# Splitting every second unit's probabilities in filled steps, with ScalarE and GpSimd sharing the work

## The chip, the cores and the metric

The kernel runs on one core of a Trainium2 chip. The metric is the device time of one execution in microseconds (us); the median of three runs is given, lowest and highest beside it. Engines go by the names of the profile: PE is TensorE with its matmuls, PEld its weight loads, DVE is VectorE, ACT is ScalarE, POOL is GpSimd, SP is SyncE, which issues most of the DMAs.

## What is computed

Two layers, each an attention block and a gated feed-forward block with a residual, over 2048 tokens of 448 features. The attention has 16 query heads of 28 features and one head of keys and values that they share. Inputs and output are f32.

```python
def _A_ref(x, wq, wk, wv, wo):
    B, S, D = x.shape
    H = 16
    Dh = D // H
    q = (x @ wq).reshape(B, S, H, Dh).transpose(0, 2, 1, 3)
    k = x @ wk
    v = x @ wv
    scores = jnp.einsum("bhqd,bkd->bhqk", q, k) * (Dh ** -0.5)
    p = _softmax(scores, axis=-1)
    o = jnp.einsum("bhqk,bkd->bhqd", p, v)
    return o.transpose(0, 2, 1, 3).reshape(B, S, H * Dh) @ wo

def _B_ref(x, w_gate, w_up, w_down):
    g = jnp.einsum("bsd,df->bsf", x, w_gate)
    u = jnp.einsum("bsd,df->bsf", x, w_up)
    return jnp.einsum("bsf,fd->bsd", _sigmoid(g) * u, w_down)

x = A_x
for _ in range(2):
    x = x + _A_ref(_layernorm(x, axis=-1), A_wq, A_wk, A_wv, A_wo)
    x = x + _B_ref(_layernorm(x, axis=-1), B_w_gate, B_w_up, B_w_down)
```

## The kernel before

**Tiles and steps.** The queries are cut into 16 tiles `u` of 128 rows, the keys into 16 tiles `kt` of 128 rows. A step, or unit, is one pair (u, kt) with all 16 heads: a layer has 256 of them. The heads go in four groups `g` of four. For a unit, four times (once for each group): a score matmul on PE (line 565) into a PSUM tile `s`, and an exponential on ACT (line 569) into an SBUF tile `P` of 128 keys by 512 (four heads of 128 queries), in f32. Then the PV matmuls of the unit (function `pv`) add the values, weighted by `P`, to one PSUM tile `pv`, whose four quarters of 32 rows belong to the four groups; the four groups' matmuls stand at different column positions of the array. Row 28 of a quarter gets the sum of the probabilities, since a column of the values is one.

**Two forms of PV.** Most units go through the f32 form: one f32 matmul for each group (line 583; the chip's records have two for each). Some units are split: each `P` is written as a sum of two f16 parts, high and low, made by `convert`. GpSimd makes the high part by a copy to f16 (line 602) and the low part by subtracting it from `P` (line 603); both go into a tile `PH`. PV is then three f16 matmuls for each group (line 579): high by high, high by low and low by high of probabilities and values; the values are split once for each layer (`VH`). Splitting is marked by the lists `KS` and the number `FROM`: a unit is split if its kt is 0, 4, 8 or 12, if 80 steps are past, and if the current order is FULL.

**Orders.** The engines get their instructions in an order that is written out by hand. A string of letters makes two steps:

```python
FULL = "FSFSFSFSTPPXMFSFSFSFSFXM"
LEAN = "FSFSmFSFSPTXmFSFSmFSFSPTXm"
```

S is a score and its exponential, followed by a call of `convert` for the tile marked before; P is the PV of the oldest waiting unit, if more than one waits; M is a group of mx work, which finds the maxima for a tile of queries ahead (four matmuls of line 508 and four reductions on DVE, line 511); F is a slice of filler work: the feed-forward block of earlier tiles (lines 369 and 787, with a tanh on ACT, line 750, a copy on ACT, line 761, and two operations on DVE, lines 758 and 762), projections for the next layer, the output projection (line 696). X moves the step on and runs short side chains, such as the normalisation of a finished tile of queries (GpSimd's multiplication of line 674 by `lb`, which comes back by DMA). FULL is used while enough filler work is left (more than 600 units of cost a step), LEAN else. In FULL the first half (up to PP) has an even kt, the second half an odd one, and both PV of the string stand together in the middle, so a unit is used up one string after its scores. What follows calls one FULL string a filled order.

**Buffers.** `P` tiles of kt divisible by four come from a pool of four (tag PX), the others from a pool of eight (tag P). Scores, mx and all filler accumulators share seven PSUM banks. The pool `big` has five SBUF tiles of 128 by 7 by 512 in f16, which hold the inputs of the projections and, early on, weights in preparation.

Behind each layer's last step comes a tail with the feed-forward block of the last tiles.

Of the kernel before, what the change touches and what calls it, by code (L numbers as in the profile page):

```python
# [8 lines left out]
F32 = mybir.dt.float32  # L9
F16 = mybir.dt.float16  # L10
I32 = mybir.dt.int32
AF = mybir.ActivationFunctionType
OP = mybir.AluOpType
# [6 lines left out]
def interleaved_layers_kernel(ctx: ExitStack, tc: tile.TileContext, x, wq, wk, wv, wo, wg, wu, wd, out, layers=2):  # L20
# [6 lines left out]
    nc = tc.nc  # L27
# [3 lines left out]
    NT, NB, G, KT, FC = S // 128, S // 512, H // 4, S // 128, F // 128  # L31
    U = NT
    TB, WB, HB = 2, 4, 8
    PB, PX = 8, 4
    HP = 2
    KS = (0, 4, 8, 12)
    FROM = 80
    CA = "PPPP"
    NBL = NT // TB
    EPS = 1e-5  # L40

# [3 lines left out]
    big = ctx.enter_context(tc.tile_pool(name="big", bufs=5))  # L45
    lay = ctx.enter_context(tc.tile_pool(name="lay", bufs=2))
    wk1 = ctx.enter_context(tc.tile_pool(name="wk1", bufs=2))
# [38 lines left out]
    def flush(every=False):  # L86
        todo, pend[:] = pend[:], []
        for i, (due, fn) in enumerate(todo):
            if due > now[0] and not every:
                pend.append((due, fn))  # L90
            else:
                fn()
        if every and pend:
            flush(True)
# [285 lines left out]
    KK, VV, VH, QH = {}, {}, {}, {}  # L380

    def layer_tiles(l):
        KK[l] = lay.tile([128, 2, S], F16, tag="KK", name="KK")
        VV[l] = lay.tile([128, KT, 32], F32, tag="VV", name="VV")
        nc.vector.memset(VV[l][:, :, 28:32], 0.0)
        nc.vector.memset(VV[l][:, :, 28:29], 1.0)
        VH[l] = lay.tile([128, 2, KT // HP, 32], F16, tag="VH", name="VH", bufs=1)
# [61 lines left out]
    def qgen(l, b):  # L449

        XT = XTQ.pop((l, b))
        for g in range(G):
            yield from qproj(l, XT, b, g)
        flush(True)
# [99 lines left out]
    def finish():  # L554
        while late:
            late.pop(0)()

    def group(m):
        next(m, None)
        next(m, None)  # L560

    def scores(l, u, kt, g, P):
        assert ("m", l, u) in stored, (l, u, kt)
        s = psf.tile([128, 512], F32, tag=BANKS["s"], name="s", bufs=NBK[BANKS["s"]])
        nc.tensor.matmul(s, KK[l][0:96, 0, kt * 128:(kt + 1) * 128], QS[l, u][:, g].rearrange("p h n -> p (h n)"),  # L565
                         start=True, stop=True)
        p = (wk1.tile([128, 512], F32, tag="P", name="P", bufs=PB) if kt % 4 else
             wk1.tile([128, 512], F32, tag="PX", name="P", bufs=PX))
        nc.scalar.activation(p, s, AF.Exp, scale=ESC)  # L569
        P.append(p)  # L570

    def pv(l, u, kt, P):
        if kt == 0:
            PVS[l, u] = psv.tile([128, 512], F32, tag="v", name="pv")
        v = PVS[l, u]
        if P[0].dtype == F16:
            for n, (a, c) in enumerate(((0, 0), (1, 0), (0, 1))):
                for g in range(4):
                    nc.tensor.matmul(v[32 * g:32 * g + 32], VH[l][:, a, kt // HP], P[g][:, c], start=kt + n == 0,
                                     stop=kt == KT - 1 and n == 2, tile_position=(0, 32 * g))  # L580
        else:
            for g in range(4):
                nc.tensor.matmul(v[32 * g:32 * g + 32], VV[l][:, kt], P[g], start=kt == 0, stop=kt == KT - 1,  # L583
                                 tile_position=(0, 32 * g))
        if kt == KT - 1:
            o = wk1.tile([128, 512], F32, name="pvs", bufs=1)
            nc.scalar.copy(o, v)
            PVS[l, u] = o


    def value_parts(l):
        nc.scalar.copy(VH[l][:, 0], VV[l][:, 0:KT:HP])
        nc.vector.tensor_tensor(VH[l][:, 1], VV[l][:, 0:KT:HP], VH[l][:, 0], op=OP.subtract)

    conv = []

    def convert():
        while conv:
            P, g = conv.pop(0)
            p, e = P[g], CA[g]  # L600
            h = wk1.tile([128, 2, 512], F16, name="PH", bufs=PX)
            {"A": nc.scalar.copy, "V": nc.vector.tensor_copy, "P": nc.gpsimd.tensor_copy}[e](h[:, 0], p)  # L602
            nc.gpsimd.tensor_tensor(h[:, 1], p, h[:, 0], op=OP.subtract)  # L603
            P[g] = h

    XTQ, BLK = {}, {}
    side = []
# [1 line left out]
    def later(*stages):  # L609

        side.append([stages[0][0], list(stages)])

    def tick():

        for s in list(side):
            s[0] -= 1
            if s[0] <= 0:
                flush()
                fill.run(s[1].pop(0)[1]())
                if s[1]:  # L620
                    s[0] = s[1][0][0]
                else:
                    side.remove(s)
# [287 lines left out]
    def warmth(n):  # L911
        p = psf.tile([128, 128], F32, tag="f", name="sca", bufs=NBK["f"])
        for _ in range(n):
            nc.tensor.matmul(p, one, one, start=True, stop=True)
# [209 lines left out]
    for n in range(4 * NB):  # L1124
        kb, g = divmod(n, G)
# [14 lines left out]
    FULL = "FSFSFSFSTPPXMFSFSFSFSFXM"  # L1140
    LEAN = "FSFSmFSFSPTXmFSFSmFSFSPTXm"
    PLAG = 1
# [8 lines left out]
    for l in range(layers):  # L1151
        mx = mxs[l]
        final = l + 1 == layers
        if not final:
            layer_tiles(l + 1)
        if l:
            for b in range(2, NB):
                fill.add(qgen(l, b), G * QCH)
        fill.slice(QCH)
        flush(True)  # L1160
        finish()
        group(mx)
        fill.slice(QCH)
        if l == 0:
            warmth(8)
        rate = 0.0
        PQ = []
        step = 0
        P = []
        sn = 0  # L1170
        while step < U * KT:
            order = FULL if rate > LEANR else LEAN
            for o in order:
                u, kt = divmod(step, KT)
                if o == "S":
                    su, skt = divmod(sn // 4, KT)
                    if sn < 4 * U * KT:
                        scores(l, su, skt, sn % 4, P)
                        convert()
                        if order is FULL and skt in KS and l * U * KT + step >= FROM and (sn % 4 == 0 or PARTS[0]):  # L1180
                            PARTS[0] = sn % 4 < 3
                            conv.append((P, sn % 4))
                        sn += 1
                        if sn % 4 == 0:
                            PQ.append((l, su, skt, P))
                            P = []
                elif o == "M":
                    group(mx)
                elif o == "m":
                    next(mx, None)  # L1190
                elif o == "T":
                    finish()
                elif o == "P":
                    convert()
                    if len(PQ) > (sn % 4 == 0) * PLAG:
                        pv(*PQ.pop(0))
                elif o == "X":
                    if u == 0 and kt in MORE:
                        group(mx)
                    if u and kt == 1:  # L1200
                        b = (u - 1) // TB
                        if (l, b) not in BLK:
                            BLK[l, b] = Block(l, b)
                        later(*BLK[l, b].tile(u - 1))
                    if step == 20:
                        value_parts(l)
                    if l == 0:
                        paced(step)
                    tick()
                    fed = sum(BLK[l, b].fed == TB for b in range(NBL) if (l, b) in BLK)  # L1210
                    if fed < NBL - 1:
                        rate = fill.left / max(FIRST + TB * KT * fed - step, 1)
                    else:
                        rate = max(fill.left - KEEP, 0) / (U * KT - step)
                    step += 1
                else:
                    fill.slice(rate * 2 / order.count("F"))
        convert()
        while PQ:
            pv(*PQ.pop(0))  # L1220
        flush(True)
        later(*BLK[l, NBL - 1].tile(U - 1))
        if not final:
            mxs[l + 1] = mx_gen(l + 1)
        n = done = 0
        many = 0 if final else 4 * NB + 1
        while side or pend or fill.first or done < many or final and fill.gens:
            tick()
            for _ in range(4):
                fill.slice(VS / 4)  # L1230
            n += 1
            if done < many and QDONE.get((l + 1, 0)) == G and mx_ready(l + 1, done) and (n >= EACH or done >= 4 * (NB - 1)):
                group(mxs[l + 1])
                done += 1
                n = 0
# [21 lines left out]
```

## Time and profile before

| | us |
|---|---|
| median of 3 runs (lowest, highest) | 2263.57 (2260.12, 2267.22) |
| the profiled execution's own time | 2260.52 |
| its span | 2258.7 |
| exponentials on ACT, line 569, 2048 of 599 ns | 1141.4 |
| mx reductions on DVE, line 511, 2048 of 680 ns | 1266.0 |
| score matmuls on PE, line 565, 2048 of 381 ns | 743.2 |

A row of the profile's groups names the line, the engine, the operation and the tile (out<-in), then the shapes, the count, the busy time in us, the mean of one in ns, and the idle time of the engine just before it with what ended it. A row of the waits names who waited for whom, the total in us, how many times, and the longest. A row of the timeline has the start, the length and the instruction; equal neighbours are merged and counted. Matmuls are pipelined and overlap in the records, so the time from one start to the next tells more of PE than the length of one.

### The profile page before, as it was taken

How to read it: one execution, taken by the hardware profiler on the slowest of the kernel's cores; microseconds unless marked ns; L12 is line 12 of the kernel's file. 1: busy time of each engine (PE TensorE's matmuls, PEld its weight loads, DVE VectorE, ACT ScalarE, POOL GpSimd, SP SyncE). 2: the span in 40 equal slices, each digit the busy share in tenths (PEclk: the TensorE clock that was granted, in tenths of full speed). 3: DMA queues.
4: the chain of work that ended last, by engine and by line, in shares of the span. 5: the costliest groups of instructions: out<-in, count | busy, mean ns of one | idle time of the engine just before them, and what ended most of it. 6: DMA issues, size and time to landing. Idle time of an engine off the chain costs nothing. (4 is left out here: it accounts for less than half of the span.)

```text
span 2258.7 us, 43078 instructions
## 1 busy us (share of the span) xinstructions
PE 2203.9 (98%) x16340; PEld 1048.8 (46%) x16340; DVE 1671.8 (74%) x2921; ACT 1397.9 (62%) x2568; POOL 1054.1 (47%) x1370
## 2 busy tenths in 40 slices
PE   8999999999999999999999999999999999999999
PEld 6312354444545454454573224445454544445457
DVE  7899887877778787774558887878787877878322
ACT  4677776666656666667325676666666666666631
POOL 5378452454454555556301015555545555555530
PEclk9999999999999999999999999999999999999999
DMA  6734642313323132323341113223222313232243
GB/s 160 214 98 132 203 141 62 107 62 99 112 64 99 61 98 72 99 95 89 101 137 53 29 51 108 79 85 101 65 91 67 103 57 99 78 95 89 78 108 113
DMA packets 224400, 217.53 MB, mean 96 GB/s; under 512 B 154048, under 2 KB 185536, under 8 KB 224192
## 3 DMA queue, kind: packets, MB, share of 16 engines
q1 hardware_dynamic: 217200, 198.89, 30.1%
q0 software_dynamic: 3680, 12.09, 1.4%
q10 hardware_dynamic: 3312, 3.79, 0.5%
q8 instruction: 128, 2.10, 0.4%
q14 instruction: 80, 0.66, 0.1%
HBM read 175.37 MB, written 23.59 MB: 88 GB/s over the span
## 5 line engine op out<-in xcount | busy, mean ns | idle before, releaser
L569 ACT ACTIVATE P<-s 128x512 f32<-128x512 f32 x2048 | 1141.4, 599 | 570.2 <-PE s L565 549.5
L511 DVE TENSOR_REDUCE mp<-mx 128x1 f32<-128x512 f32 x2048 | 1266.0, 680 | 308.3 <-PE mx L508 303.2
L565 PE MATMUL s<-QS,KK 96*128 96x512 f16 x2048 | 743.2, 381 | 22.2 <-DVE mp L511 9.2
L369 PEld LDWEIGHTS <-wgu 128*128 128x128 f16 x4928 | 459.4, 97 | 254.4 <-issue 92.0
L603 POOL TENSOR_TENSOR PH<-P,PH 128x512 f16<-128x512 f32 x388 | 463.9, 1196 | 31.1
L602 POOL CAST PH<-P 128x512 f16<-128x512 f32 x388 | 251.7, 649 | 474.9 <-ACT P L569 474.9
L583 PE MATMUL pv<-P,VV 128*32 128x512 f32 x3320 | 418.1, 600 | 0.0
L369 PE MATMUL gp<-XT,wgu 128*128 128x256 f16 x2464 | 386.4, 272 | 0.9 <-DVE mp L511 0.7
L369 PE MATMUL up<-XT,wgu 128*128 128x256 f16 x2464 | 385.3, 272 | 1.1 <-ACT P L569 0.4
L787 PE MATMUL dn<-WD,h 128*128 128x448 f16 x1344 | 330.4, 353 | 0.0
L508 PE MATMUL mx<-KK,QH 32*128 32x512 f16 x2048 | 256.8, 385 | 6.0 <-ACT th L750 2.2
L565 PEld LDWEIGHTS <-KK 96*128 96x128 f16 x2048 | 188.9, 97 | 135.7 <-issue 60.7
L508 PEld LDWEIGHTS <-QH 32*128 32x128 f16 x2048 | 62.1, 91 | 345.6 <-issue 342.8
L787 PEld LDWEIGHTS <-h 128*128 128x128 f16 x1344 | 124.8, 98 | 138.8 <-issue 23.8
L583 PEld LDWEIGHTS pv<-P,VV 128*32 128x32 f32 x3320 | 86.3, 109 | 169.4 <-issue 148.0
L762 DVE SCALAR_TENSOR_TENSOR h<-th,h 128x512 f16<-128x512 f32 x112 | 99.0, 884 | 48.4 <-ACT h L761 48.4
L761 ACT ACTIVATE h<-th 128x512 f16<-128x512 f32 x112 | 70.4, 628 | 82.8 <-DVE th L758 81.8
L758 DVE SCALAR_TENSOR_TENSOR th<-th,up 128x512 f32<-128x512 f32 x112 | 75.8, 677 | 57.0 <-PE up L369 51.8
L750 ACT ACTIVATE th<-gp,gsc 128x512 f32<-128x512 f32 x112 | 76.9, 686 | 43.9 <-PE gp L369 43.5
L369 PE MATMUL qp<-XT,WQ 128*128 128x512 f16 x352 | 99.4, 387 | 0.8 <-DVE ktl L412 0.7
L674 POOL TENSOR_TENSOR lb<-pvs,lb 128x512 f32<-128x512 f32 x32 | 40.7, 1273 | 124.3 <-DMA lb<-sums 99.6
L329 POOL TENSOR_SCALAR rs<-mv 128x1 f32<-128x1 f32 x48 | 11.0, 230 | 186.1 <-DVE mv L324 186.1
(163 smaller groups left out, 1103.8 us busy)
## 6 DMA issues: line engine op xcount, KB each, us to landing
wgu<-wgu_d SPq DMA_DIRECT2D x224, 512.0 KB
QS<-qd SPq DMA_DIRECT2D x384, 32.0 KB
lb<-sums SPq DMA_DIRECT2D x120, 64.0 KB
wgu_d<-sgu POOLq DMA_DIRECT2D x14, 512.0 KB, 3.8
qd<-qst POOLq DMA_DIRECT2D x16, 256.0 KB, 2.7
xr<-in_A_x_dram SPq DMA_DIRECT2D x16, 224.0 KB
QH<-qd SPq DMA_DIRECT2D x28, 128.0 KB
x2d<-x SPq DMA_DIRECT2D x16, 224.0 KB
```

The costliest lines, as they stand in the source:

```text
L369: nc.tensor.matmul(ps, a, b, start=n == 0, stop=n == 10)
L508: nc.tensor.matmul(ps[h][:, :nk], qh[32 * h:32 * h + 32, g], KK[l][32 * h:32 * h + 32, 1, ks], start=True, stop=True, tile_position=(32 * ...
L511: nc.vector.tensor_reduce(mp[:, g, h, kb:kb + 1], ps[h][:, :nk], axis=AX.X, op=OP.max)
L565: nc.tensor.matmul(s, KK[l][0:96, 0, kt * 128:(kt + 1) * 128], QS[l, u][:, g].rearrange("p h n -> p (h n)"), start=True, stop=True)
L569: nc.scalar.activation(p, s, AF.Exp, scale=ESC)
L583: nc.tensor.matmul(v[32 * g:32 * g + 32], VV[l][:, kt], P[g], start=kt == 0, stop=kt == KT - 1, tile_position=(0, 32 * g))
L602: {"A": nc.scalar.copy, "V": nc.vector.tensor_copy, "P": nc.gpsimd.tensor_copy}[e](h[:, 0], p)
L603: nc.gpsimd.tensor_tensor(h[:, 1], p, h[:, 0], op=OP.subtract)
L750: defer(lambda: nc.scalar.activation(th, gp.rearrange("p j n -> p (j n)"), AF.Tanh, scale=gsc))
L758: nc.vector.scalar_tensor_tensor(t, th, 1.0, up.rearrange("p j n -> p (j n)"), op0=OP.add, op1=OP.mult)
L762: defer(lambda: nc.vector.scalar_tensor_tensor(h[:, 1], t, 2.0 ** -17, h[:, 0], op0=OP.mult, op1=OP.subtract), 1)
L787: nc.tensor.matmul(p, hs[f // 2][:, a, o:o + 128], WD[:, f, c], start=n == 0, stop=n == 3 * FC - 1)
```

## The change

Every second kt is on the list instead of every fourth, so in a filled order every first half is split. Three of the four high parts are made by ACT, the first by GpSimd as before; all low parts stay on GpSimd. The four high parts and three of the low parts of a unit go into one tile of the pool `big`, the fourth low part into a new small tile `PL`; the old `PH` tiles are gone. The `P` tiles of even kt come from the pool PX, now of seven, those of odd kt from the pool of eight. The limit on waiting units at the letter P is written in another way.

```diff
@@ -31,11 +31,11 @@
-    PB, PX = 8, 4
+    PB, PX = 8, 7
     HP = 2
-    KS = (0, 4, 8, 12)
+    KS = range(0, 16, 2)
     FROM = 80
-    CA = "PPPP"
+    CA = "PAAA"
@@ -564,7 +564,7 @@
-        p = (wk1.tile([128, 512], F32, tag="P", name="P", bufs=PB) if kt % 4 else
+        p = (wk1.tile([128, 512], F32, tag="P", name="P", bufs=PB) if kt % 2 else
              wk1.tile([128, 512], F32, tag="PX", name="P", bufs=PX))
@@ -573,10 +573,10 @@
-        if P[0].dtype == F16:
+        if isinstance(P[0], tuple):
             for n, (a, c) in enumerate(((0, 0), (1, 0), (0, 1))):
                 for g in range(4):
-                    nc.tensor.matmul(v[32 * g:32 * g + 32], VH[l][:, a, kt // HP], P[g][:, c], start=kt + n == 0,
+                    nc.tensor.matmul(v[32 * g:32 * g + 32], VH[l][:, a, kt // HP], P[g][c], start=kt + n == 0,
                                      stop=kt == KT - 1 and n == 2, tile_position=(0, 32 * g))
@@ -592,16 +592,21 @@
-    conv = []
+    conv, ph = [], [None]
 
     def convert():
         while conv:
             P, g = conv.pop(0)
             p, e = P[g], CA[g]
-            h = wk1.tile([128, 2, 512], F16, name="PH", bufs=PX)
-            {"A": nc.scalar.copy, "V": nc.vector.tensor_copy, "P": nc.gpsimd.tensor_copy}[e](h[:, 0], p)
-            nc.gpsimd.tensor_tensor(h[:, 1], p, h[:, 0], op=OP.subtract)
-            P[g] = h
+            if g == 0:
+                ph[0] = big.tile([128, 7, 512], F16, tag="big", name="PH")
+            hi = ph[0][:, g]
+            lo = ph[0][:, 4 + g] if g < 3 else wk1.tile([128, 512], F16, name="PL", bufs=2)
+            {"A": nc.scalar.copy, "V": nc.vector.tensor_copy, "P": nc.gpsimd.tensor_copy}[e](hi, p)
+            nc.gpsimd.tensor_tensor(lo, p, hi, op=OP.subtract)
+            P[g] = hi, lo
+            if g == 3:
+                ph[0] = None
@@ -1192,7 +1197,7 @@
                 elif o == "P":
                     convert()
-                    if len(PQ) > (sn % 4 == 0) * PLAG:
+                    if len(PQ) > (PLAG if order is FULL or sn % 4 == 0 else 0):
                         pv(*PQ.pop(0))
```

The first place is ACT's queue in layer 1, from the copy of a finished `pv` tile (line 587) on. Rows stand in the order of issue, with the count of equal neighbours; L569 is the exponential, L750 and L755 are the tanh, L761 and L766 the copy to `h`. Before:

```order
L587 COPY pvs<-pv 128x512
L569 ACTIVATE P<-s 128x512 x6
L750 ACTIVATE th<-gp,gsc 128x512
L569 ACTIVATE P<-s 128x512 x8
L761 ACTIVATE h<-th 128x512
```

And after, the same stretch, with the new copies of line 605:

```order
L587 COPY pvs<-pv 128x512
L569 ACTIVATE P<-s 128x512 x6
L755 ACTIVATE th<-gp,gsc 128x512
L569 ACTIVATE P<-s 128x512
L605 CAST PH<-P 128x512
L569 ACTIVATE P<-s 128x512
L605 CAST PH<-P 128x512 x2
L569 ACTIVATE P<-s 128x512 x6
L766 ACTIVATE h<-th 128x512
```

Between the third and the fourth exponential of a first half there is now one copy, and behind the fourth there are two; the rest of the queue is as it was.

The second place is POOL's queue in the same layer, ahead of the multiplication by `lb` of a tile of queries. Before, one split unit:

```order
L602 CAST PH<-P 128x512
L603 TENSOR_TENSOR PH<-P,PH 128x512
L602 CAST PH<-P 128x512
L603 TENSOR_TENSOR PH<-P,PH 128x512
L602 CAST PH<-P 128x512
L603 TENSOR_TENSOR PH<-P,PH 128x512
L602 CAST PH<-P 128x512
L603 TENSOR_TENSOR PH<-P,PH 128x512
L674 TENSOR_TENSOR lb<-pvs,lb 128x512
```

After, the last two split units ahead of the same multiplication:

```order
L605 CAST PH<-P 128x512
L606 TENSOR_TENSOR PH<-P,PH 128x512 x3
L606 TENSOR_TENSOR PL<-P,PH 128x512
L605 CAST PH<-P 128x512
L606 TENSOR_TENSOR PH<-P,PH 128x512 x3
L606 TENSOR_TENSOR PL<-P,PH 128x512
L679 TENSOR_TENSOR lb<-pvs,lb 128x512
```

A unit has one copy instead of four on POOL and as many subtractions, and there are twice as many units.

The third place is PE's queue at a PV pair that has no split unit before. Before, between the last score of a first half (line 565) and the mx matmuls (line 508):

```order
L565 LDWEIGHTS KK
L565 MATMUL s<-QS,KK 128x512
L583 MATMUL pv<-P,VV 32x512 x8
L508 LDWEIGHTS QH
L508 MATMUL mx<-KK,QH 128x512
```

After, the end of the twelve f16 matmuls of the unit that is split now, and the other unit:

```order
L579 MATMUL pv<-PH,VH 32x512
L579 LDWEIGHTS VH
L579 MATMUL pv<-PL,VH 32x512
L583 MATMUL pv<-P,VV 32x512 x4
L508 LDWEIGHTS QH
L508 MATMUL mx<-KK,QH 128x512
```

Four f32 matmuls of the pair have become twelve f16 ones. In the whole program the f16 PV matmuls go from 1164 to 2328, the f32 ones from 1660 to 1272, the copies of ACT from none to 582; GpSimd's copies go from 388 to 194 and its subtractions from 388 to 776. All other instructions keep their order on every engine.

## The prediction

> **What bounds the kernel now.** I read the page first, its busy times and its 40 slices, to find the engine that is never free.
>
> ```profile
> PE 2203.9 (98%) x16340; PEld 1048.8 (46%) x16340; DVE 1671.8 (74%) x2921; ACT 1397.9 (62%) x2568; POOL 1054.1 (47%) x1370
> ...
> PE   8999999999999999999999999999999999999999
> ...
> ACT  4677776666656666667325676666666666666631
> POOL 5378452454454555556301015555545555555530
> PEclk9999999999999999999999999999999999999999
> ```
>
> PE is busy in every slice, at full clock, while ACT and POOL have a third and a half of the span free. The change reaches only the two stretches in which units are already split: the f16 PV matmuls of line 579 begin at 396.9 us and end at 2163.1 us, with a gap between the layers. So I took the windows 385 to 1062 us (layer 0) and 1355 to 2170 us (layer 1) for the busy time of each engine, and the waits of PE, ACT and POOL in them.
>
> ```profile
> L579 PE MATMUL pv<-PH,VH x1164: 376/379/390, 396.9 to 2163.1; 128*32 128x512 f16 x194
> 385.00:1062.00 677.00, 665.52 (x5138) 324.75 (x5140) 516.64 (x886) 439.47 (x799) 361.64 (x496) 1.00 0.30 88
> 1355.00:2170.00 815.00, 810.91 (x6239) 396.93 (x6238) 602.79 (x1003) 533.20 (x961) 432.59 (x540) 1.00 0.29 86
> PE s L565 <- ACT P L569: 0.9, 4, 0.2
> PE s L565 <- ACT P L569: 1.6, 6, 0.3
> ACT P L569 <- PE s L565: 198.3, 198, 2.9
> ACT P L569 <- PE s L565: 231.5, 205, 3.2
> POOL PH L602 <- ACT P L569: 201.3, 33, 9.3
> POOL PH L602 <- ACT P L569: 269.3, 39, 9.4
> ```
>
> Behind a window stand its length and the busy time of PE, PEld, DVE, ACT and POOL. PE has 665.5 + 810.9 = 1476.4 of 1492 us, 99%. Its score matmuls wait for ACT 0.9 and 1.6 us in all, while ACT waits 198.3 + 231.5 = 429.8 us for scores and POOL 201.3 + 269.3 = 470.6 us for exponentials. So here the time is the sum of what PE is given, and less PE work shortens the span as long as the two engines that are given more stay inside their idle time. The tails behind the stretches hold no probabilities and stay as they are.
>
> **The change part by part.** *What goes from PE.* In the filled order the PV matmuls of two units stand together, and the PE timeline shows both kinds of pair: a split unit with an f32 unit, and two f32 units. What counts is the time from the pair's start to the start of the mx matmuls behind it.
>
> ```profile
> 1003.12 0.83 PE L579 MATMUL pv<-PH,VH 128*32 128x512 f16 x12
> 1003.78 1.03 PE L583 MATMUL pv<-P,VV 128*32 128x512 f32 x8
> 1004.74 0.40 PE L508 MATMUL mx<-KK,QH 32*128 32x512 f16 x4
> ...
> 1615.95 1.92 PE L583 MATMUL pv<-P,VV 128*32 128x512 f32 x16
> 1617.81 0.40 PE L508 MATMUL mx<-KK,QH 32*128 32x512 f16 x4
> ```
>
> The mixed pair takes 1004.74 - 1003.12 = 1.62 us, the f32 pair 1617.81 - 1615.95 = 1.86 us, so a unit that becomes split saves 0.24 us. (Spans of single matmuls overlap, four side by side, and can't be added.) Today 1164 / 12 = 97 units are split, those of every second filled order. With the new list it is every filled order: the changed program has 2328 such matmuls, 194 units, 97 more. **Saved on PE: 97 x 0.24 = 23.3 us.** Everything else on PE keeps its place.
>
> *What ScalarE gets.* Three of the four high parts of all 194 units: 582 copies. The nearest row is a copy of the same shape and types on ACT.
>
> ```profile
> L680 ACT CAST oT<-lb 128x512 f16<-128x512 f32 x32 | 19.6, 613 | 14.8 <-POOL lb L674 14.8
> ```
>
> 582 x 0.613 = 357 us, or 1.84 us in each of 194 orders, which take 1492 / 194 = 7.69 us on average. ACT has 439.5 + 533.2 = 972.7 us in the windows; with the copies 1330 of 1492 - 23 = 1469 us, 91%. On average that fits into the 429.8 us in which it waits for scores. But its queue is in order, and the copies come in a bunch: one ahead of the fourth exponential of the order's first half, two behind it. What stands behind them is the first exponential of the second half. The ACT timeline of one order shows the place.
>
> ```profile
> 1618.87 2.27 ACT L569 ACTIVATE P<-s 128x512 f32<-128x512 f32 x4 [0.33 <-PE s L565]
> 1622.02 1.08 ACT L569 ACTIVATE P<-s 128x512 f32<-128x512 f32 x2 [0.88 <-PE s L565]
> 1623.00 0.68 ACT L750 ACTIVATE th<-gp,gsc 128x512 f32<-128x512 f32 x1
> 1623.57 1.09 ACT L569 ACTIVATE P<-s 128x512 f32<-128x512 f32 x2
> 1626.20 2.41 ACT L569 ACTIVATE P<-s 128x512 f32<-128x512 f32 x4 [1.54 <-PE s L565]
> 1629.32 1.15 ACT L569 ACTIVATE P<-s 128x512 f32<-128x512 f32 x2 [0.71 <-PE s L565]
> ```
>
> The four exponentials of 1622.02 to 1624.66 are a first half, with a tanh among them; then ACT is idle for 1.54 us, while PE does the PV pair. Three copies of 0.613 fill that and 0.30 us more, and the next gap, 0.71 us, takes up the rest before the following order. Without a tanh there the gap is longer by its 0.68 us. So exponentials start late by a few tenths of a microsecond, and only in the second halves; PE feels it where a score, or an mx, needs the PSUM bank that such an exponential still reads. There are seven banks for all of them. The bounds: nothing (all hidden), and the whole overshoot of 0.30 us in every order, 194 x 0.30 = 58 us. I take a value near the lower end, 0.02 us an order, 4 us in all, because the tanh stands in this very place today, delays two exponentials by 0.68 us, and PE's scores wait for ACT only 2.5 us in both windows together.
>
> Another place is worse. When a layer's maxima are finished, orders have no mx matmuls and are shorter, while ACT's part stays.
>
> ```profile
> 1040.00:1090.00 50.00, 50.00 (x409) 27.27 (x410) 11.53 (x21) 37.95 (x75) 34.49 (x47) 1.00 0.39 109
> 2110.00:2165.00 55.00, 55.00 (x426) 29.21 (x418) 8.77 (x14) 39.22 (x74) 32.88 (x41) 1.00 0.39 109
> ```
>
> ACT has 37.95 + 39.22 = 77.2 of 105 us here, with 75 + 74 instructions; eight an order are exponentials and, with one more for the rest, these are some 16 orders (an estimate from that count). The copies add 16 x 1.84 = 29.4 us: 106.6 us of work on ACT, against 105 - 8 x 0.24 = 103 us on PE. **ACT sets the end there, and costs about 3 us.**
>
> *What GpSimd gets and loses.*
>
> ```profile
> L603 POOL TENSOR_TENSOR PH<-P,PH 128x512 f16<-128x512 f32 x388 | 463.9, 1196 | 31.1
> L602 POOL CAST PH<-P 128x512 f16<-128x512 f32 x388 | 251.7, 649 | 474.9 <-ACT P L569 474.9
> ```
>
> A split unit cost it 4 x (0.649 + 1.196) = 7.38 us every second order and costs 0.649 + 4 x 1.196 = 5.43 us every order now. In the windows: 361.6 + 432.6 - 97 x 7.38 + 194 x 5.43 = 1132 of 1469 us, 77%. A unit's four low parts can be done about 6.3 us after its first exponential (an exponential, then 5.43), and PV asks for them an order and a half's exponentials later, 7.69 + 2.64 = 10.3 us; the 4 us between are the cover for what else GpSimd's queue holds: the normalisation (lb, line 674), the rstd chain, the hl parts, each behind a wait for a DMA or DVE. I cost it at nothing; if the cover is gone, PE stands at a PV matmul, which today happens for 0.6 us twice. A new wait goes the other way: seven PX tiles for four an order mean that an order's fourth exponential needs the first low part of the order before, which has more than 5 us to spare, and that keeps it at nothing too.
>
> One rule speaks against this. DVE's line 762, which reads two tensors of SBUF, takes this long:
>
> ```profile
> L762 DVE SCALAR_TENSOR_TENSOR h<-th,h x112: 676/693/1606, 282.4 to 2240.5; 128x512 f16<-128x512 f32 x112
> L762 DVE SCALAR_TENSOR_TENSOR h<-th,h 128x512 f16<-128x512 f32 x112 | 99.0, 884 | 48.4 <-ACT h L761 48.4
> ```
>
> Its median is 693 ns, its mean 884 and its longest 1606. GpSimd is busy 53% of the windows today and 77% after; if the 191 ns between mean and median grow with that share, they become 277 ns, and 112 x 0.086 is 10 us of DVE time in all. DVE has 516.6 + 602.8 = 1119 of 1492 us in the windows, so I put this at nothing for the sum and keep it as a rival. The Trainium skill, in the GPSIMD Engine Reference, section Specifications, says that GpSimd shares its SBUF interfaces with VectorE and contends with DVE instructions that have two SBUF inputs; the long line-762 instructions are in accord with it. By that page the change would hurt DVE, and by the rows it has the room.
>
> *What does nothing.* The new condition on PQ: in the filled order eight scores are issued with PV behind the fourth, so the count is a multiple of four there, and the old and the new limit are both one. The tiles from the big pool: two live at once, and the input tiles of the next layer leave that many. Their price is nothing; without that, GpSimd's first copy would wait.
>
> **The sum**, against the profiled execution (2260.5 us, span 2258.7 and 1.8 around it): 2260.5 - 23.3 + 4 + 3 = 2244.2. That execution lies 3 us under the median of the three runs, 2263.6, which spread from 2260.1 to 2267.2; I add half the distance and forecast **2246 us**.
>
> **The rivals.**
> 1. *Everything is hidden.* ACT's copies fit in all places, and the PSUM banks carry the late exponentials: 2260.5 - 23.3 = 2237, to 2240. For it: ACT's 429.8 us of waiting for 357 us of copies. Against it: the orders without mx, above.
> 2. *ACT paces PE in part.* At 91% in order, with a tanh or a copy for pvs, oT, hl in the same half, PE waits 0.1 us in each of 194 orders, 19 us, and the saving is eaten: 2253 to 2266. For it: the overshoot of 0.30 us in the row above; against it: PE's 2.5 us of waits for ACT.
> 3. *DVE is slowed* by GpSimd's low parts and passes its 10 us to PE through the mx banks: 2254. Against it: 75% busy.
> 4. *Slower.* The overshoot is passed on whole. The second half's exponentials begin 0.30 us late, PE's scores have no free bank because mx holds four of seven, and each order ends late: 2260.5 - 23.3 + 58 = 2295. The point from which it makes the kernel slower is 23.3 / 194 = 0.12 us an order. Against it: the gap of 0.71 us behind that half, which takes up such a lag before the next order.
>
> That the change doesn't do what it says is left no chance: the program has the 194 units.
>
> **How the numbers follow.** The forecast (2241 to 2252) gets 0.43, all hidden 0.17, ACT in part 0.22, DVE 0.04, slower 0.14. The range runs from 2236, all hidden, to 2266, the upper end of ACT in part, and leaves out what lies above. A measurement can tell about 0.3% from no change, 6.8 us, so faster means under 2256.8: the first two cases, a third of ACT in part and half of DVE's, 0.69. Within 0.3%: the rest of both and a little of the slower case, 0.20. Slower: 0.11.
>
> **What would show it.** Right: mixed pairs of 1.62 us in every filled order, ACT near 1755 us and POOL near 1390 us busy, PE's waits for ACT under 10 us in the windows, PE still at 98%. Wrong: PE's score matmuls waiting long for P of line 569 (rivals 2 and 4), PV waiting for PH or PL (GpSimd late), exponentials waiting for POOL (the PX tiles), or DVE's line 762 near 1 us with PE waiting for mp (rival 3). The forecast fails if the orders, 7.69 us now, don't become about 0.1 us shorter.

## The result, and the profile after

| | median us | lowest to highest | runs |
|---|---|---|---|
| before | 2265.39 | 2260.12 to 2267.86 | 4 |
| after | 2290.89 | 2289.28 to 2298.52 | 4 |

The ratio of after to before is 1.0116, with an interval of 1.0096 to 1.0135. The change makes the kernel 1.2% slower; the forecast was 2246 us, with a range up to 2266. The profiled execution after took 2292.15 us (span 2290.4), 31.6 us more than the one before (2260.52).

The page of after, its busy times and slices (before's stand in the prediction):

```profile
PE 2208.6 (96%) x16728; PEld 1059.3 (46%) x16728; DVE 1722.0 (75%) x2921; ACT 1673.5 (73%) x3150; POOL 1379.9 (60%) x1564
...
PE   8999999999999999999999999999999999999999
...
ACT  4677866787778788878514678878787888878851
POOL 4377452776667776778502017777777776777750
PEclk8999999999999999999999999999999999999999
```

The slices show a bound PE, as before, and neither ACT nor GpSimd full. Two things don't fit the plan. PE's busy time grew by 4.7 us, though it got 23.3 us less to do: a busy PE here is one whose records overlap, also while single matmuls start late. And DVE, which the change gives nothing, has 50.2 us more busy time with the same 2921 instructions. The two windows of the prediction, now of after (us, then PE, PEld, DVE, ACT, POOL, clock, DMA share, GB/s):

```profile
385.00:1062.00 677.00, 648.45 (x5129) 318.23 (x5128) 539.89 (x880) 536.87 (x1008) 482.69 (x553) 0.99 0.29 84
1355.00:2170.00 815.00, 802.58 (x6327) 388.96 (x6326) 637.46 (x1029) 674.41 (x1257) 589.05 (x628) 1.00 0.28 84
```

PE's idle time went from 11.5 to 28.6 us in the first and from 4.1 to 12.4 us in the second. The waits of after, first window, then second:

```profile
ACT P L569 <- PE s L565: 114.3, 161, 2.8
PE s L565 <- DVE mp L511: 22.8, 33, 1.9
ACT P L569 <- POOL PL L606: 3.5, 3, 1.2
PE s L565 <- ACT P L569: 0.9, 4, 0.2
...
ACT P L569 <- PE s L565: 114.8, 149, 3.3
PE s L565 <- DVE mp L511: 6.3, 11, 0.8
ACT P L569 <- POOL PL L606: 5.9, 5, 1.2
PE s L565 <- ACT P L569: 3.4, 13, 0.3
```

The same wait before, which had no such row in the second window:

```profile
PE s L565 <- DVE mp L511: 5.9, 16, 0.5
```

So scores of layer 0 wait for DVE's reductions, 22.8 us instead of 5.9. The reductions themselves are as long as before, 681 ns in the median against 680. What grew on DVE stands in its groups and, in the first row below, in the minimum, median and maximum of one line's instructions. After:

```profile
L345 DVE CAST hl<-xn x32: 393/1229/1235, 198.7 to 2226.2; 128x448 f16<-128x448 f32 x32
L345 DVE CAST hl<-xn 128x448 f16<-128x448 f32 x32 | 33.5, 1046 | 1.1
L347 DVE TENSOR_TENSOR hl<-xn,hl 128x384 f16<-128x384 f32 x16 | 19.5, 1221 | 0.0
L353 DVE TENSOR_SCALAR xn<-x,mv,rs 128x448 f32<-128x448 f32 x48 | 30.7, 640 | 12.7 <-POOL rs L334 12.7
L767 DVE SCALAR_TENSOR_TENSOR h<-th,h 128x512 f16<-128x512 f32 x112 | 101.9, 910 | 53.2 <-ACT h L766 53.2
```

Before:

```profile
L345 DVE CAST hl<-xn x32: 393/394/844, 195.4 to 2194.5; 128x448 f16<-128x448 f32 x32
L345 DVE CAST hl<-xn 128x448 f16<-128x448 f32 x32 | 13.4, 419 | 1.1
L347 DVE TENSOR_TENSOR hl<-xn,hl 128x384 f16<-128x384 f32 x16 | 8.8, 550 | 0.0
L353 DVE TENSOR_SCALAR xn<-x,mv,rs 128x448 f32<-128x448 f32 x48 | 24.9, 518 | 13.8 <-POOL rs L334 13.7
```

The copy to f16 of a normalised tile (line 345) took 394 ns in the median and takes 1229; the subtraction of line 347 went from 550 to 1221. Line 767 (762 before), the only one that the prediction weighed, grew by 26 ns, from 884. The timeline of after shows what a long one does:

```profile
399.71 3.42 POOL L606 TENSOR_TENSOR PH<-P,PH 128x512 f16<-128x512 f32 x3
...
401.79 0.31 DVE L346 TENSOR_TENSOR hl<-xn,hl 128x64 f16<-128x64 f32 x1 [1.91 <-ACT hl L345]
...
402.02 1.53 DVE L347 TENSOR_TENSOR hl<-xn,hl 128x384 f16<-128x384 f32 x1
...
403.09 1.47 POOL L606 TENSOR_TENSOR PL<-P,PH 128x512 f16<-128x512 f32 x1
403.47 1.87 DVE L511 TENSOR_REDUCE mp<-mx 128x1 f32<-128x512 f32 x3
404.20 0.38 PE L565 MATMUL s<-QS,KK 96*128 96x512 f16 x1 [0.89 <-DVE mp L511]
```

GpSimd subtracts the whole time; DVE's line 347 takes 1.53 us; the reductions queue behind it, and PE stands idle for 0.89 us until the score, whose PSUM bank still holds an mx tile, can start. The other kind of stall, in layer 1 of after, has ACT in that place:

```profile
1659.49 0.61 ACT L605 CAST PH<-P 128x512 f16<-128x512 f32 x1
...
1659.99 0.60 ACT L569 ACTIVATE P<-s 128x512 f32<-128x512 f32 x1
1660.48 1.13 ACT L605 CAST PH<-P 128x512 f16<-128x512 f32 x2
...
1661.51 1.58 ACT L569 ACTIVATE P<-s 128x512 f32<-128x512 f32 x3
...
1662.17 0.38 PE L565 MATMUL s<-QS,KK 96*128 96x512 f16 x1 [0.27 <-ACT P L569]
...
1662.80 0.71 PE L508 MATMUL mx<-KK,QH 32*128 32x512 f16 x4
```

After the two copies the second half's exponentials start at 1661.51, the first frees its bank at 1662.11, and the score takes it at 1662.17. The group of four mx takes 0.71 us here instead of 0.39 or 0.40: its last matmul needs the bank of the third exponential, which ends at 1663.09. The view of waits doesn't list that at all, since PE isn't idle then. **So the waits alone undercount.**

**A ledger of stalls.** I therefore counted in the traces, for the two filled stretches: where a PSUM tile's first matmul starts within 150 ns of the end of the last read of its bank's former tile, how much later it starts than the usual distance from the matmul before it; and who made that last read, DVE's reductions (line 511) or ACT's exponentials (line 569). A third column has the time of the mixed PV pairs above 1.62 us, summed. All in us; "sum" is what they add up to over before's, less 23.3 us where 97 units more are split (11.5 us for 48 in e11); "measured" is the ratio less one, of 2264 us.

| kernel | DVE | ACT | PV | sum | measured |
|---|---|---|---|---|---|
| before | 23.2 | 6.5 | 3.1 | | |
| after | 52.9 | 25.2 | 8.3 | +30.3 | +26.3 |
| e1, ACT copies alone, 97 units | 28.8 | 13.2 | 0.9 | +10.1 | +10.6 |
| e2, after, DVE relieved | 27.5 | 21.4 | 8.3 | +1.1 | +3.6 |
| e3, before + GpSimd dummies | 48.5 | 7.2 | 14.9 | +37.8 | +43.2 |
| e4, before + three ACT dummies | 19.5 | 30.5 | 4.2 | +21.4 | +25.1 |
| e5, after, copies behind | 47.7 | 25.1 | 7.4 | +24.1 | +25.4 |
| e6, e2 + copies spread | 39.8 | 36.8 | 31.6 | +52.1 | +57.1 |
| e7, after, copies spread | 51.5 | 38.7 | 31.6 | +65.7 | +68.4 |
| e8, before, DVE relieved | 21.6 | 6.7 | 3.2 | -1.3 | +1.6 |
| e9, e2, two copies on ACT | 25.3 | 8.6 | 35.2 | +13.0 | +13.6 |
| e10, e2 + e5 | 22.3 | 22.5 | 8.0 | -3.3 | -1.8 |
| e11, e2, GpSimd alone, 145 units | 21.2 | 8.0 | 87.7 | +72.6 | +76.5 |
| e12, e2, GpSimd alone, 194 units | 27.5 | 33.5 | 116.1 | +120.9 | +122.9 |
| e13, e2, copies two and one | 24.5 | 12.7 | 25.7 | +6.8 | +11.1 |
| e14, before + two ACT dummies | 23.9 | 14.1 | 3.3 | +8.5 | +14.9 |

For after it says: 29.7 us from DVE, 18.7 from ACT, 5.2 from late parts, less the 23.3 that were saved. The experiments below move the columns apart, and for all fifteen kernels the sum comes to within 7 us of the measured difference.

The columns stand for one traced execution of each kernel, "measured" for all its runs. Since times follow the granted clock (last section), the clock is a rival for a part of the differences. A straight line through the 54 runs of before that were taken beside the experiments falls by 1.6 us for each 0.001 of clock. At their own clocks, after's four runs lie 23.0 to 25.3 us above this line; on average e1's lie 10.5 above, e2's 1.0, e3's 40.2, e14's 8.1, and e10's 3.7 below. So by this estimate the clock makes some 2 of after's 26.3 us, and the rest is the kernel's own.

### The profile page after: what moved, and what is told of

Its sections match the earlier page's. It is cut to its first block, busy times and chain, and to the rows that moved or that the text cites. A ratio compares the mean times of both kernels' runs of the same rounds, so it can differ in the third digit from the quotient of the medians.

```text
span 2290.4 us, 44477 instructions
## 1 busy us (share of the span) xinstructions
PE 2208.6 (96%) x16728; PEld 1059.3 (46%) x16728; DVE 1722.0 (75%) x2921; ACT 1673.5 (73%) x3150; POOL 1379.9 (60%) x1564
## 5 line engine op out<-in xcount | busy, mean ns | idle before, releaser
L569 ACT ACTIVATE P<-s 128x512 f32<-128x512 f32 x2048 | 1150.5, 604 | 359.0 <-PE s L565 324.6
L606 POOL TENSOR_TENSOR PH<-P,PH 128x512 f16<-128x512 f32 x582 | 691.3, 1211 | 33.6 <-ACT PH L605 16.6
L605 ACT CAST PH<-P 128x512 f16<-128x512 f32 x582 | 343.1, 630 | 0.0
L583 PE MATMUL pv<-P,VV 128*32 128x512 f32 x2544 | 334.6, 601 | 0.0
L508 PE MATMUL mx<-KK,QH 32*128 32x512 f16 x2048 | 268.6, 384 | 9.0 <-ACT th L755 2.7
L605 POOL CAST PH<-P 128x512 f16<-128x512 f32 x194 | 118.2, 609 | 244.4 <-ACT P L569 244.3
L606 POOL TENSOR_TENSOR PL<-P,PH 128x512 f16<-128x512 f32 x194 | 228.7, 1179 | 0.0
L579 PE MATMUL pv<-PH,VH 128*32 128x512 f16 x2134 | 162.8, 384 | 0.9 <-POOL PH L606 0.9
L766 ACT ACTIVATE h<-th 128x512 f16<-128x512 f32 x112 | 70.6, 630 | 81.8 <-DVE th L763 80.9
L583 PEld LDWEIGHTS pv<-P,VV 128*32 128x32 f32 x2544 | 69.7, 109 | 99.7 <-issue 61.0
```

The lines of the kernel that those rows point to most:

```text
L508: nc.tensor.matmul(ps[h][:, :nk], qh[32 * h:32 * h + 32, g], KK[l][32 * h:32 * h + 32, 1, ks], start=True, stop=True, tile_position=(32 * ...
L606: nc.gpsimd.tensor_tensor(lo, p, hi, op=OP.subtract)
```

## The experiments

Times are medians, ratios are to the kernel before on the same chip, with intervals.

**Each suspect alone.** e1 is the kernel before with the new division of the copies: 97 units as before, three of four high parts on ACT.

```diff
-    CA = "PPPP"
+    CA = "PAAA"
```

> The kernel before with one edit: three of the four high parts are made by ACT (CA = PAAA); the split units stay the 97 of before. Theory D (DVE is held up behind GpSimd's subtractions, and PE's scores wait for the PSUM banks of DVE's maxima): GpSimd gets less, the subtractions stay; 2259 to 2266 us, no worse than before. Theory A (ACT's copies stand ahead of exponentials whose PSUM banks PE needs): half of the orders have copies; if ACT is all of the loss of about 45 us, 2280 to 2290 us; if it is some 18 of the 45, about 2274.

2276.43 us, 1.0047 (1.0030 to 1.0064): slower with less work on GpSimd and none saved on PE. 291 copies on ACT cost some 10 us, 36 ns each. In the ledger 6.7 us of it are ACT's and 5.6 DVE's; DVE's stand for the most part behind its line 681, whose mean went from 988 to 1162 ns; why it did the runs don't show. Theory D's "no worse than before" failed; 2274 us, for an ACT share of some 18 of 45 us, was near.

e3 gives GpSimd's extra subtractions to the kernel before, four on constants in every second filled order, and nothing to ACT. Their results, like those of the ACT dummies in e4 and e14, go nowhere.

```diff
+            if P is None:
+                src, hi, junk = dummy()
+                nc.gpsimd.tensor_tensor(junk, src, hi, op=OP.subtract)
+                continue
...
+                        if order is FULL and skt % 4 == 2 and l * U * KT + step >= FROM:
+                            conv.append((None, sn % 4))
```

> The kernel before, with four more subtractions of 128x512 on GpSimd in every second filled order, on a tile of constants; nothing uses their result, and ACT gets nothing new. GpSimd so makes as many subtractions as in the changed kernel. Theory D: about 25 to 30 us more than before, 2288 to 2296 us. Theory A: nothing, 2262 to 2268 us.

2308.33 us, 1.0191 (1.0175 to 1.0206). Its windows:

```profile
385.00:1062.00 677.00, 653.85 (x4979) 315.51 (x4976) 540.77 (x881) 423.70 (x768) 537.84 (x634) 0.99 0.29 84
1355.00:2170.00 815.00, 801.78 (x6053) 380.00 (x6052) 637.13 (x1031) 523.53 (x940) 643.89 (x719) 1.00 0.27 82
```

And DVE's groups in it:

```profile
L353 DVE TENSOR_SCALAR xn<-x,mv,rs 128x448 f32<-128x448 f32 x48 | 44.0, 917 | 16.7 <-POOL rs L334 16.7
L345 DVE CAST hl<-xn 128x448 f16<-128x448 f32 x32 | 33.4, 1044 | 1.1
L347 DVE TENSOR_TENSOR hl<-xn,hl 128x384 f16<-128x384 f32 x16 | 8.8, 548 | 0.0
```

DVE's busy time in the windows, 540.8 and 637.1 us, is that of after (539.9 and 637.5), with not one instruction of DVE or ACT changed: GpSimd's subtractions stretch DVE's instructions, and which of them depends on what meets (line 353 more here, line 347 not). DVE's column in the ledger grows by 25.3 us, after's by 29.7. Another 11.8 us come from PV, since GpSimd is behind with the real parts, so the 43 us are more than the DVE route is worth.

e4 and e14 give ACT's copies to the kernel before, again on constants: e4 all three at the change's places, e14 only two, behind the fourth exponential.

```diff
+            if P is None:
+                src, hi, junk = dummy()
+                nc.scalar.copy(junk, src)
+                continue
...
+                        if order is FULL and skt % 2 == 0 and l * U * KT + step >= FROM and sn % 4:
+                            conv.append((None, sn % 4))
```

In e14 the last condition is `sn % 4 > 1`.

> The kernel before, with three more copies of 128x512 to f16 on ACT in every filled order, at the places of the change, from a tile of constants; nothing uses their result, and GpSimd gets nothing new. Theory D: 0 to 5 us more than before, 2265 to 2270 us. Theory A: about 18 us more, 2283 us, or up to 2310 us if ACT is all of the loss.

> The kernel before, with two copies of constants on ACT in every filled order, both behind the fourth exponential; nothing uses their result. If a copy that fits the gap costs nothing: 2264 to 2268 us. If ACT's loss goes by the sum of its work: two thirds of the 17 to 28 us that three such copies cost, 2276 to 2283 us.

e4 took 2291.93 us, 1.0111 (1.0079 to 1.0144), e14 2280.23 us, 1.0066 (1.0040 to 1.0092). Both medians are soft: their runs lie 18 us apart and follow the granted clock (last section). And both traces hold two costs that are no copy's. Counted by the starts of the exponentials against before's, 14.3 us of e4's loss and 8.9 us of e14's stand ahead of the first dummy. Then this first dummy waits until GpSimd has filled the tile of constants, in e4 and in e14:

```profile
408.21 0.62 ACT L609 CAST dm<-dm 128x512 f16<-128x512 f32 x1 [5.38 <-POOL dm L600]
...
404.60 1.27 ACT L609 CAST dm<-dm 128x512 f16<-128x512 f32 x2 [6.57 <-POOL dm L600]
```

Over this single wait the exponentials fall behind by another 5.9 and 6.0 us. What comes after it, up to the last exponential, is the price of the copies in these two traces: 17.6 us for three in an order, 4.5 us for two. So three cost, and two behind the fourth exponential cost little. e14's time fits the theory of two thirds only by luck, through the two other costs. (By the ledger three dummies add 24.0 us of stalls behind ACT and two add 7.6; both have the stalls of that single wait in them.)

**Each suspect taken away.** e2 is after, with DVE relieved: the copies of line 345 go to ACT, the subtractions of lines 346 and 347 to GpSimd.

```diff
-                v["hl"] = ln_split(self.x1[:, t], *v["ls"], eng=nc.gpsimd)
+                v["hl"] = ln_split(self.x1[:, t], *v["ls"], eng=nc.gpsimd, hi=nc.scalar.copy)
...
-                v["hl"] = ln_split(v["x2"], *v["ls"], eng=nc.vector, hi=nc.scalar.copy)
+                v["hl"] = ln_split(v["x2"], *v["ls"], eng=nc.gpsimd, hi=nc.scalar.copy)
```

> The changed kernel with the operations that stretched most on DVE moved away: the f16 copy of the normalised rows (line 345 behind the output projection) goes to ACT, the two subtractions of lines 346 and 347 behind the down projection go to GpSimd. Theory D: about 25 us of the stalls go, 2264 to 2272 us. Theory A: nothing is gained, and ACT has 32 more copies, 2290 to 2296 us.

2267.50 us, 1.0016 (1.0006 to 1.0025): of after's 1.16%, 1.00% is gone, 22.6 us, which the two intervals fix to some 5 us either way. In the waits of e2, first window, the scores' row is near before's 5.9 us again:

```profile
PE s L565 <- DVE mp L511: 6.8, 14, 0.8
```

Its groups show where the work went:

```profile
L347 POOL TENSOR_TENSOR hl<-xn,hl 128x384 f16<-128x384 f32 x48 | 46.8, 976 | 0.0
L345 ACT CAST hl<-xn 128x448 f16<-128x448 f32 x48 | 27.5, 572 | 56.2 <-DVE xn L353 56.2
```

e8 makes the same moves in the kernel before, to see if they are worth anything by themselves.

> The kernel before with the same moves of DVE's work. Its GpSimd makes half of the subtractions. If the moves pay by the contention with GpSimd: 3 to 8 us less than before, 2256 to 2261 us. If they pay simply since DVE has less to do: about 23 us less, as in the changed kernel, 2240 us.

2267.16 us, 1.0007 (0.9991 to 1.0022): nothing, not the 3 to 8 us that contention with half of the subtractions was expected to cost either. The 22.6 us are thus not a gain of another kind that e2 happened on, but the price of those instructions beside the extra subtractions. **DVE's hold-up is shown from both sides**: added alone in e3, taken away in e2, void in e8.

e5 takes the copy between the third and the fourth exponential of after away from there; all three stand behind the fourth. e10 does that in e2.

```diff
-                        convert()
+                        if sn % 4 < 2:
+                            convert()
```

> The changed kernel, with all three copies of ACT behind the fourth exponential of the first half, and none ahead of it. If ACT's part of the loss is that the copy ahead delays the fourth exponential, whose PSUM bank the mx matmuls behind the PV pair take, most of some 13 us goes: 2276 to 2282 us. If it is the bunch of three ahead of the second half's first exponential, nothing goes: 2288 to 2294 us.

> The run with relief of DVE, with all three copies of ACT behind the fourth exponential. By the waits of mx in the run with copies behind, 3 to 6 us less than with relief alone: 2261 to 2265 us. If the place of the first copy is nothing: 2267 us.

e5 took 2289.28 us, 1.0112 (1.0084 to 1.0140): no difference from after that can be told, and the ledger's ACT column stays at 25. e10 took 2264.03 us, 0.9992 (0.9979 to 1.0005), against e2's 1.0016: some 0.2% less. It is the best version found, and by its median no faster than before (3.7 us faster at equal clock, by the line above). Its waits, second window:

```profile
ACT P L569 <- PE s L565: 84.7, 130, 2.7
...
PE s L565 <- ACT P L569: 3.9, 12, 0.4
PE s L565 <- DVE mp L511: 1.0, 2, 0.7
```

DVE is out of it. ACT's column is still 16.0 us above before's, and with PV's 4.9 us that takes most of the 23.3.

**Other places for the parts.** If copies in a bunch are late for the second half, they might be spread: one behind the fourth exponential, one behind the sixth, one behind the seventh. e6 does so in e2, e7 in after.

```diff
-    def convert():
-        while conv:
+    def convert(most=99):
+        for _ in range(min(most, len(conv))):
...
-                        convert()
+                        if order is not FULL:
+                            convert()
+                        elif sn % 4 == 1 or sn % 8 == 6:
+                            convert(1)
...
-                    convert()
+                    convert(len(conv) // 3 if order is FULL else 99)
```

> The moves of DVE's work as in the run with relief, and ACT's three copies spread over the order: one behind the fourth exponential, one behind the sixth, one behind the seventh. If the two losses are separate and add up: 2248 to 2258 us, below the kernel before. If one of them contains the other: 2263 to 2268 us, as with relief alone.

> The changed kernel with ACT's copies spread as above and DVE's work as it was. If the place of the copies matters and not their sum: 2272 to 2279 us. If it is ACT's load as such: 2288 to 2294 us.

Both miss by far: 2319.79 us, 1.0252 (1.0227 to 1.0276), and 2332.48 us, 1.0302 (1.0277 to 1.0328). Copies among the second half's exponentials hold those up (ACT 37 and 39 in the ledger), and GpSimd, which needs the high parts, gets them later, so that PV waits (31.6). The difference of the two, 11 us, is in DVE's column (51.5 and 39.8): half of what the same relief gave in e2, and why e6's column stays that high the runs don't show.

e9 (two copies on ACT, both behind the fourth exponential, two on GpSimd) and e13 (two behind the fourth, one behind the eighth) take less from ACT in that place. e11 and e12 take all from ACT; e11 splits 6 of 16 kt, e12 all 8. All four have e2's moves.

```diff
-    CA = "PAAA"
+    CA = "PPAA"
...
-                        convert()
+                        if sn % 4 < 3:
+                            convert()
```

e13's edit is in convert's calls:

```diff
-                        convert()
+                        if order is not FULL or sn % 8 in (1, 7):
+                            convert()
...
-                    convert()
+                    convert(max(len(conv) - 1, 0) if order is FULL else 99)
```

And e11's, of which e12 has the second line alone:

```diff
-    KS = range(0, 16, 2)
+    KS = (0, 2, 4, 8, 10, 12)
...
-    CA = "PAAA"
+    CA = "PPPP"
...
-        p = (wk1.tile([128, 512], F32, tag="P", name="P", bufs=PB) if kt % 2 else
+        p = (wk1.tile([128, 512], F32, tag="P", name="P", bufs=PB) if kt not in KS else
```

> The run with relief of DVE, with two of the high parts on GpSimd and two on ACT, both behind the fourth exponential: 1.23 us, which fits the gap of 1.54 us behind a first half. If ACT's part of the loss comes from copies that make exponentials late: 2252 to 2260 us, below before. If it goes by the sum of ACT's work: two thirds of some 18 us stay, 2260 to 2264 us. If GpSimd, with 5.90 us an order, is late for PV: above 2267 us.

> The run with relief of DVE; of ACT's three copies two stand behind the fourth exponential (1.23 us, for a gap of 1.54) and one behind the eighth (0.61 us, for a gap of 0.71). If the loss by ACT is the part of the copies that doesn't fit the gap they stand in: 2250 to 2258 us, below before. If it goes by the sum of ACT's work, which is the same: 2262 to 2266 us. If the last low part is late for PV: 2266 us or more, with PE waiting for PL.

> The run with relief of DVE, with all high parts on GpSimd and units split at kt 0, 2, 4, 8, 10 and 12 (145 units): ACT gets no copy. If the two losses found (DVE behind GpSimd, exponentials behind copies) are all there is: saving 48 x 0.24 = 11.5 us against before, some 3 us of other DVE work held up, 2254 to 2260 us. If GpSimd is late in the pairs of split orders in a row: PE waits at PV, 2266 us or more.

> The run with relief of DVE, with all four high parts on GpSimd in all 194 units: 7.38 us of 7.69 us an order, behind the rest of its queue. If GpSimd's time is the bound: PE waits at PV for the parts, 2300 us or more. If only the two losses found count: 2245 to 2252 us.

e9 took 2280.79 us, 1.0060 (1.0040 to 1.0080), e13 2277.37 us, 1.0049 (1.0031 to 1.0067), e11 2342.76 us, 1.0338 (1.0317 to 1.0359), e12 2388.45 us, 1.0543 (1.0521 to 1.0564). In e9 and e13 ACT's column falls to 8.6 and 12.7, which is what they were made for, and PV's rises to 35 and 26. The waits of PV, e9's:

```profile
PE pv L579 <- POOL PL L606: 19.1, 28, 0.7
```

e13's:

```profile
PE pv L579 <- POOL PL L606: 9.5, 18, 1.4
```

e12's:

```profile
PE pv L579 <- POOL PH L605: 40.9, 37, 1.7
PE pv L579 <- POOL PL L606: 28.5, 50, 0.9
```

All four took the branch of their expectations in which GpSimd is late. One copy more an order on GpSimd, or one high part half an order later, and the last low part misses PV. (Why e12, with no copy on ACT, has 33.5 us in ACT's column I did not follow up.) Of the divisions tried, the change's own, three high parts on ACT and one on GpSimd, is the best; none hides the work of both engines.

## Why the prediction was wrong, step by step

- **PE saves 23.3 us: right.** After has 194 mixed pairs, still 1.62 us in the median. The place where before had the f32 pair of 1.86 us, in the PE timeline of after:

```profile
1625.99 0.83 PE L579 MATMUL pv<-PH,VH 128*32 128x512 f16 x11
...
1626.65 1.03 PE L583 MATMUL pv<-P,VV 128*32 128x512 f32 x8
1627.62 0.39 PE L508 MATMUL mx<-KK,QH 32*128 32x512 f16 x4
```

The pair takes 1627.62 - 1625.99 = 1.63 us.

- **DVE at nothing: the step that failed.** The prediction weighed line 762 alone, grew its excess with GpSimd's share to 10 us of DVE time, and put that at nothing because "by the rows it has the room". The time that it named for that route was 2254. DVE's busy time rose by 50 us, 20.1 of them on line 345 and 10.7 on line 347; line 767 has 2.9. And DVE's room did not count, for a reduction behind a stretched instruction keeps a PSUM bank from PE at that moment: 29.7 us in the ledger, 22.6 by e2 against after. The place agrees. A count of such stalls that leaves out the banks' order has 49 us of them in after and 22 in before; the longest DVE instruction on SBUF tiles that ended in the 4 us ahead is one of lines 345 to 347 for 26 of the 49 and for 0.3 of the 22. Before's own trace had the hint, a copy at 394 ns in the median with a maximum of 844. The Trainium skill's GPSIMD Engine Reference, section Specifications, names two kinds of DVE instructions that contend with GpSimd, those with two SBUF inputs and those in a 2-port mode; the prediction used only the first. VectorE: DVE Perf Modes, in the section "Why PSUM operands drop a tier", says that operands in PSUM can't have the 2-port mode. The rows are in accord with that: what grew reads SBUF, with one input (lines 345, 353) or two (line 347), and reductions from PSUM grew not at all. Not everything that reads SBUF grew: line 323, which reads `x` for the normalisation, stays at 628 ns. That the ports are the cause is the pages' account; the runs show the effect alone.
- **ACT at 4 us in the orders with mx: mis-sized.** The place was right (first exponentials of the second half, PE's mx and scores behind them), the size was 18.7 us in the ledger, 0.10 us in each of 194 orders; that is rival 2's 0.1 us an order and its 19 us. ACT's waits for scores, 429.8 us, didn't protect: 229.1 us of them are still there. The step that misled was to take PE's 2.5 us of named waits for ACT as the measure of what PE feels; mx matmuls that start late don't appear there. ACT's load was not underestimated: its busy time ended at 1673.5 us and not near 1755, since the copies' records overlap their neighbours' (two take 1.13 us).
- **ACT at 3 us where a layer's maxima are finished: the time by luck, the engine wrong.** The 75 scores behind each layer's last mx take 128.2 us in the two layers of after together and 126.5 before, 1.7 us more where PE got some 2 us less to do. But no tile's first matmul is over 30 ns late behind an exponential there. PE stands in one PV pair of each layer, which takes 3.41 and 3.74 us instead of 1.62, because GpSimd did the rstd chain of a row's normalisation (lines 329 to 334) ahead of that unit's parts. The one in layer 0:

```profile
1103.52 0.38 PE L579 MATMUL pv<-PH,VH 128*32 128x512 f16 x1 [0.31 <-POOL PH L606]
1104.63 0.38 PE L579 MATMUL pv<-PL,VH 128*32 128x512 f16 x1 [0.74 <-POOL PL L606]
```

- **GpSimd's lateness and the PX tiles at nothing: a few us off.** PV's pairs lost 5.2 us, 3.9 of them in the two pairs above. Exponentials waited for a PX tile, 9.4 us in eight places, and PE is idle beside one of the eight alone, for 0.14 us. The cover of 4 us (an exponential of 0.60 and 5.43 us make 6.0 us, not 6.3, so 4.3) was thin: the rstd chain used it up twice, and e9 and e13 did so often.
- **`big`, and the limit on waiting units, at nothing:** nothing speaks against it.
- **Rival 4 had the sign and nearly the time (2295) by the wrong mechanism:** ACT's overshoot was not passed on whole. ACT alone would have taken the change to about no gain (e10, 0.9992); with DVE's share it became slower.

What stays open: the traces give DVE 29.7 us and the removal 22.6, and e1, e4 and e10 don't fix ACT's share closer than some 5 us.

## What to carry to other kernels

Before giving GpSimd more elementwise work on SBUF tiles, look at the minimum, median and maximum of every DVE instruction that reads SBUF, copies too: a spread there is a sign of the price, and it is paid by what queues behind, so DVE's share of busy time doesn't show it. Where two engines return the PSUM banks that a bound engine needs, idle time on average is no room for work ahead of those returns in an in-order queue; what counts is the gap at that place, which held two copies at 4.5 us in all and three at 17.6. And count late starts from one matmul's start to the next: a busy PE and a short list of waits can hide them.

## What the runs showed of the hardware

- A DVE copy of 128x448 from f32 to f16 takes 394 ns, and 1229 ns in the median in the trace with twice GpSimd's subtractions of 1.16 us each; reductions of 128x512 from PSUM stay at 680 and 681 ns (all medians).
- Times of one kernel follow its mean granted clock: e8's runs go from 2258.30 us at 0.996 to 2275.18 us at 0.989, some 2.4 us for each 0.001; the line through before's 54 runs has 1.6. e4 took 2298.23 us at 0.989 and 2280.26 at 0.995, e14 2288.15 at 0.987 and 2270.29 at 0.995. Eight of the ten runs of these two were at 0.992 or less, the 54 runs of before beside the experiments at 0.990 to 0.998. In the traces the missing clock is short stretches at half of it: e4 has 0.50 from 107.4 to 127.8 us and e14 from 108.6 to 125.6 us, long ahead of the first dummy, where before has 1.00; each has another at 0.50, of 6.8 us, right behind the wait for the constants. Why the early ones come in some runs and not in others is open.
